# A dilated gated convolution: the last 16 channels summed by token, one of four products split further, and a new order of all steps

## The chip, the core and the metric

The kernel runs on one core of a Trainium2 chip. Its engines work side by side, each through its own queue in order: TensorE (PE in the profile, its weight loads PEld), VectorE (DVE), ScalarE (ACT), GpSimd (POOL), and SyncE (SP), which here only issues DMAs. They tell each other of finished work by semaphores. The metric is device time of one execution in microseconds; lower is better.

## The reference

```python
B, T, D, K = 2, 16000, 144, 15
dil, pad = 2, (K - 1) * 2
xp = jnp.pad(x, ((0, 0), (pad, 0), (0, 0)))
h = sum over i of einsum('btc,cd->btd', xp[:, pad - 2*i : pad - 2*i + T], w[i])   # w[i]: 144 x 288
z = jnp.tanh(h[..., :D]) * sigmoid(h[..., D:])
return z @ w_o                                                                    # w_o: 144 x 144
```

A causal convolution with 15 taps, each 2 tokens apart, from 144 to 288 channels; a gate; a projection. Everything is bf16, sums are held in f32.

## The kernel before, in words

Even and odd tokens never meet in the convolution, so each parity is a plane of its own with taps 1 apart. Per plane there are 8000 positions per batch, cut into groups of 24 positions. A block is 128 groups of one plane; there are 10 such blocks, and a last block of 32 groups of both planes. `load_x` brings the first 128 channels of a block to SBUF with a transposing DMA (channels on partitions); `gather` copies the last 16 channels to a DRAM tensor `xr`, and `load_r` reads that with overlapping rows, so that one transposing DMA puts 8 taps times 16 channels on 128 partitions (`rx`).

A unit is 12 of a group's 24 positions for all 128 groups, so there are 20 units (r is 0 or 1) and one for the last block. With 12 outputs and 15 taps a unit is computed as four smaller products, named S, D, F and G, from sums and differences of inputs 8 or 16 apart. F and G give outputs 8 to 11 and 0 to 3 together with U = (S + D)/2, and (S − D)/2 is outputs 4 to 7. The names S, D, E are also those of the sums on VectorE (`derive`, line 271), E serving F and G; a 2 or a 4 behind the name is a sum of neighbours 2 or 4 apart, an r is the same over `rx`.

Each product (`conv`) is again split, over taps 4 apart and then 2 apart, in these steps, which the plan knows by name:

- VV: 2 matmuls into one half of a PSUM pair X. cVV (line 507): ACT copies it negated into the other half.
- V2a, V2b: 2 matmuls on each half. cV (line 513): ACT copies both halves, negated, into another pair Y.
- A: for each of the four halves of X and Y, 4 matmuls (3 where a tap is missing) with the 128-channel sums, and 1 with the r sums.

Every matmul has 128 x 128 inputs as weights and 288 columns of w. There are four PSUM pairs in all, handed out in the order of the plan. For S and D the pairs are evicted by ACT into `m` (line 570), and VectorE makes y of outputs 4 to 7 and U from `m`; for F and G VectorE adds the pair to U (y) and so frees it. A gate is tanh, sigmoid and a product (z) over four outputs, three gates per unit. z is transposed by a DMA (`zT`, line 603), and the projection (OP0, OP1, line 343) is 24 matmuls with 144 columns, evicted by ACT into `os` (line 678) and stored.

All of this is written down as steps with a cost, the steps they depend on, and a `want`, a due time. `Plan.place` is a list scheduler: it goes through the engines with these costs and takes, among the steps that could start soonest, the one with the smallest `want`; so it sets the order on PE, ACT and DVE and who gets which PSUM pair. In the kernel before, `want` is worked out from a table of a unit's sequence (`SEQ`) and a unit length TU of 14.0. Transfers from SP are issued in an order that the scheduler of the framework may still move, except those held in program order.

For the last block ACT first spreads the inputs out (`spread_out`, line 328, 8 copies), so that groups of both planes stand side by side.

The prologue loads w, makes sums of taps (G1, Gm, H, HH: partly on VectorE, line 407, partly on TensorE by matmuls with the identity, `psum_sum`), and runs 48 matmuls on zeros. Unit 0 has an order of its own.

Of the kernel before, what the change touches and what calls it, by code (L numbers as in the profile page):

```python
# [11 lines left out]
ALU = mybir.AluOpType  # L12
# [14 lines left out]
def t_dve(n, psum=False):  # L27
    return 0.07 + n / (960 if psum else 1920)

# [32 lines left out]
class Plan:  # L62
# [4 lines left out]
    def __init__(self, n_slots):  # L67
        self.steps, self.n_slots = [], n_slots

    def add(self, eng, cost, fn, r=(), w=(), u=(), want=0.0, opens=None, pairs=(), name="", lat=None, behind=()):  # L70
# [3 lines left out]
        s.idx = len(self.steps)  # L74
# [15 lines left out]
        s.deps, s.behind = deps, set(behind) - deps  # L90
        for p in pairs:
            p.users.append(s)
        self.steps.append(s)
        return s

# [57 lines left out]
def kernel(  # L153
# [25 lines left out]
    TU = 14.0  # L179
# [36 lines left out]


    xn_b, rx_b = buf("xn", [P, XW], 2), buf("rx", [P, XW], 2)
    xr = dram.tile([2, NPOS, CR], BF16, name="xr")
    xr_g = {}  # L220
    blk = [dict() for _ in blocks]

    def plane(t_, bi, i):
        _, n, _, _ = geometry(bi)
        return t_[:, i * (HA + n):(i + 1) * (HA + n)]

    def load_x(bi, want, half=None, behind=()):

        p0, n, planes, _ = geometry(bi)
        if half != 1:  # L230
            blk[bi]["xn"] = xn_b.new(bi)
        g = blk[bi]["xn"]
        if half is not None:
            blk[bi]["xn", half] = Gen(g.before)
        gs = [g] if half is None else [g, blk[bi]["xn", half]]
        a, m = (0, HA + n) if half is None else ((0, HA + n // 2), (HA + n // 2, n // 2))[half]
        for i, e in enumerate(planes):
            v = plane(g.tile, bi, i)[:, a:a + m]
            loads, zeros = runs(p0 - HA + a, m)
            for c, m in zeros:  # L240
                add("POOL", 0.2, lambda v=v, c=c, m=m: nc.gpsimd.memset(v[:, c:c + m], 0.0), w=gs, want=want)
            for c, b, p, m in loads:
                src = bass.AP(x.tensor, x[b, 2 * p + e, 0].offset, [[2 * D, m], [1, P]])
                add("DMA", m * 0.0015, lambda v=v, c=c, m=m, src=src: nc.sync.dma_start_transpose(out=v[:, c:c + m], in_=src),
                    w=gs, want=want, name="xn", behind=behind)

    def gather(key, p0, n, planes, want, behind=()):
        g = xr_g[key] = Gen()
        loads, _ = runs(p0, n)
        for c, b, p, m in loads:  # L250
            e0, ne = planes[0], len(planes)
            src = bass.AP(x.tensor, x[b, 2 * p + e0, P].offset, [[2 * D, m], [D, ne], [1, CR]])
            dst = bass.AP(xr.tensor, xr[e0, FRONT + p0 + c, 0].offset, [[CR, m], [NPOS * CR, ne], [1, CR]])
            add("DMA", m * ne * 0.0013, lambda dst=dst, src=src: nc.sync.dma_start(out=dst, in_=src), w=[g], want=want, name="gather", behind=behind)

    def load_r(bi, want, keys):
        p0, n, planes, _ = geometry(bi)
        g = blk[bi]["rx"] = rx_b.new(bi)
        for i, e in enumerate(planes):
            v = plane(g.tile, bi, i)  # L260
            src = bass.AP(xr.tensor, xr[e, FRONT + p0 - HA - 7, 0].offset, [[CR, HA + n], [1, P]])
            add("DMA", (HA + n) * 0.0015, lambda v=v, src=src: nc.sync.dma_start_transpose(out=v, in_=src),
                r=[gz, *(xr_g[k] for k in keys)], w=[g], want=want, name="rx")
# [3 lines left out]
           "S2": (-4, 6), "D2": (-4, 6), "E2": (-12, 14), "Sr": (0, 8), "Dr": (0, 8), "Er": (-8, 16)}  # L267
    DER_B = {nm: buf(nm, [P, P * GEO[nm][1]], 2 if nm in ("E", "S4", "D4", "E4", "E2", "Er") else 1) for nm in GEO}

    def tt(out_, a, b, op):  # L270
        return K_(nc.vector.tensor_tensor(out=out_, in0=a, in1=b, op=op))  # L271

    def derive(bi, nm, want, half=None):
# [5 lines left out]
        k0, kn = (0, ns) if half is None else (half * (ns // 2), ns // 2)  # L279

        last = len(planes) == 2

        def cols(v, c, *dims):
            v = v[:]
            return bass.AP(v.tensor, v.offset + c, [list(v.ap[0]), *[list(d) for d in dims]])

        def go(g=g):
            if nm[-1] in "42":
                b0, bw = GEO[nm[0]]
                v, d = blk[bi][nm[0]].tile, int(nm[-1])  # L290
                a = [cols(v, (u0 - b0) * (ns if last else 1) + q, *([[1, wd * ns]] if last else [[bw, kn], [1, wd]])) for q in ((0, d * ns) if last else (k0 * bw, k0 * bw + d))]
                tt(cols(g.tile, 0, [1, wd * ns]) if last else cols(g.tile, k0 * wd, [wd, kn], [1, wd]), a[0], a[1], ALU.add)
                return
            t_ = blk[bi]["rx" if nm[-1] == "r" else "xn"].tile
            us = (u0, u0 + (16 if nm[0] == "E" else 8))
            if last:
                first = -8 if nm[-1] == "r" else -16
                lo, hi, o = *(cols(spread[nm[-1] == "r"], (u - first) * ns, [1, wd * ns]) for u in us), cols(g.tile, 0, [1, wd * ns])
            else:
                lo, hi = (cols(t_, HA + u + k0 * PU, [PU, kn], [1, wd]) for u in us)  # L300
                o = cols(g.tile, k0 * wd, [wd, kn], [1, wd])
# [5 lines left out]
        of = blk[bi][nm[0] if nm[-1] in "42" else "rx" if nm[-1] == "r" else "xn"]  # L307
        if last and nm[-1] not in "42":
            of = spread_g[nm[-1] == "r"]
        if half is not None and ("xn", half) in blk[bi]:  # L310
            of = blk[bi]["xn", half]
        add("DVE", t_dve(kn * wd), go, r=[of], w=[g], want=want, name=nm)

    spread = [const.tile([P, 40 * 64], BF16, name="xs"), const.tile([P, 32 * 64], BF16, name="rs")]
    spread_g = [Gen(), Gen()]

    def spread_out(bi, want):

        _, n, _, ns = geometry(bi)
        for i, (key, first, wd) in enumerate((("xn", -16, 40), ("rx", -8, 32))):  # L320
            for h in range(4):
                m = wd // 4

                def go(i=i, key=key, u=first + m * h, m=m, h=h):
                    a, b = blk[bi][key].tile[:], spread[i][:]
                    src = bass.AP(a.tensor, a.offset + HA + u, [list(a.ap[0]), [1, m], [HA + n, 2], [PU, ns // 2]])
                    dst = bass.AP(b.tensor, b.offset + h * m * ns, [list(b.ap[0]), [ns, m], [ns // 2, 2], [1, ns // 2]])
                    K_(nc.scalar.copy(out=dst, in_=src))  # L328

                add("ACT", t_act(m * ns), go, r=[blk[bi][key]], w=[spread_g[i]], want=want + 4 * i + h, name="spread")  # L330

    def stat(bi, r, nm, u):

        u0, wd = GEO[nm]
        v = blk[bi][nm].tile[:]
        ns = geometry(bi)[3]
        step, c = (1, (u - u0) * ns) if r is None else (wd, u - u0 + r)
        return bass.AP(v.tensor, v.offset + c, [list(v.ap[0]), [step, P]])
# [11 lines left out]
    HH = const.tile([P, 4, 2, D2], BF16)  # L350
    Wr = const.tile([P, 4, D2], BF16)
# [23 lines left out]
    zr = const.tile([64, 2, P], BF16)  # L375
    K_(nc.gpsimd.memset(zr[:], 0.0))
# [3 lines left out]


    gz = Gen()
    for q, (p0, m) in enumerate(((-FRONT, FRONT), (HP, GAP), (ENDP, NPOS - FRONT - ENDP))):
        dst = bass.AP(xr.tensor, xr[0, FRONT + p0, 0].offset, [[P, m * CR // P], [NPOS * CR, 2], [1, P]])
        add("ACT", 0.08, lambda dst=dst, m=m: nc.scalar.dma_start(out=dst, in_=zr[0:m * CR // P]), w=[gz], want=-30.5 if q == 0 else -25, lat=2.5)
# [50 lines left out]
    for i, k in enumerate("SD"):  # L436
# [4 lines left out]
        if k == "D":  # L441
# [4 lines left out]
            wsum(HH[:, i], H[:, i, 0:2], H[:, i, 2:4], ALU.subtract, [gH[k]], [gHH[k]], 0.9)  # L446
            continue
        psum_sum(HH[:, i], [plus(i, j) + minus(i, j + 4) + minus(i, j + 2) + plus(i, j + 6) for j in range(2)], wall, [gHH[k]], wt)
        psum_sum(H[:, i, 0:2], [plus(i, j) + minus(i, j + 4) for j in (0, 1)], wall, [gH[k]], wt + .2)
        psum_sum(H[:, i, 2:4], [plus(i, j) + minus(i, j + 4) for j in (2, 3)], wall, [gH[k]], wt + .1)  # L450
        psum_sum(g[:, 4:6], [plus(i, j) for j in (4, 5)], wall, [gG[k, 1]], wt + .3)
# [8 lines left out]


    y_b, m_b, U_b = buf("y", [P, NCL, D2], 2), buf("m", [P, 2, 4, D2], 2), buf("U", [P, 4, D2], 2)
    th_b, sg_b = buf("th", [P, 4, D], 3), buf("sg", [P, 4, D], 3)
# [3 lines left out]
    for z_ in z_b.tiles:  # L467
# [4 lines left out]
    SEQ = (("A0S", 1.22), ("V2D", .49), ("A1S", 1.22), ("VVF", .25), ("A0D", 1.22), ("V2F", .49), ("A1D", 1.22), ("VVG", .25),  # L472
           ("OP0", .75), ("A0F", 1.22), ("V2G", .49), ("A1F", 1.22), ("VVS'", .25), ("OP1", .75), ("A0G", 1.1), ("V2S'", .49),
           ("A1G", 1.22), ("VVD'", .25))
    SEQ0 = (("VVF", .25), ("VVG", .25), ("V2F", .49), ("A0F", 1.22), ("V2G", .49), ("A1F", 1.22), ("VVS", .25), ("A0G", 1.1),
            ("V2S", .49), ("A1G", 1.22), ("VVD", .25), ("A0S", 1.22), ("V2D", .49), ("A1S", 1.22), ("A0D", 1.22), ("VVS'", .25),
            ("A1D", 1.22), ("V2S'", .49), ("VVD'", .25), ("OP0", 0), ("OP1", 0))
# [9 lines left out]
    AT_ = {False: times(SEQ), True: times(SEQ0[:15] + (SEQ0[16],))}  # L487
# [320 lines left out]
```

## Time and profile before

| | us |
|---|---|
| median of 3 runs | 355.1 (354.83 to 355.15) |
| the profiled execution | 352.94 |
| its span, first to last instruction | 351.1 |
| PE, ACT, DVE busy in it | 324.0, 255.1, 243.5 |
| granted TensorE clock, mean | 0.988 |

A row of the timeline is start, length, engine, line, operation and out<-in with sizes; in brackets stands how long the engine was idle before it and what ended that. A row of a group ends in busy time, mean nanoseconds of one, idle time before them and its releasers. Matmuls overlap, so the length of one is longer than the step to the next; the step is what counts.

### The profile page before, as it was taken

Reading aid. Unit: us, or ns where it says so; the run is one execution under the profiler, and the core shown is the slowest. Engines: PE = TensorE matmul, PEld = TensorE weight load, DVE = VectorE, ACT = ScalarE, POOL = GpSimd, SP = SyncE. Lnnn points to the kernel's source line nnn. Section 1 sums busy time; section 2 is a strip of 40 time slices with the busy share of each in tenths; the row PEclk is TensorE's granted clock in tenths of the full one; section 3 lists DMA queues with packets and bytes.
Section 4 is the critical chain, followed back from the end, with each engine's and each line's share of the span. In section 5 each row is a group of like instructions: output and inputs, shape, how many; then the busy total and the mean of one; then the engine's idle time right before and its main releaser. Section 6 shows DMA issues by size and latency. Waiting matters only on the chain.

```text
span 351.1 us, 6812 instructions
## 1 busy us (share of the span) xinstructions
PE 324.0 (92%) x2754; PEld 302.7 (86%) x2754; DVE 243.5 (69%) x336; ACT 255.1 (73%) x448; POOL 21.8 (6%) x52
## 2 busy tenths in 40 slices
PE   8988596999999999999999999999988899999992
PEld 3678595899999899989989989998987889999881
DVE  3778966398697768939848794894877387385352
ACT  1256864686887687777677876767779997788883
POOL 8780000000000000000000000000000000000000
PEclk9999899999999999999999999999999999999996
DMA  9999999219349616426920833794090242202144
GB/s 192 225 82 62 117 212 192 52 40 193 54 169 191 109 21 141 93 54 246 191 54 1 149 86 85 204 200 54 1 140 0 54 202 54 54 1 54 29 131 157
DMA packets 140700, 38.17 MB, mean 109 GB/s; under 512 B 136995, under 2 KB 139347, under 8 KB 140670
## 3 DMA queue, kind: packets, MB, share of 16 engines
q1 hardware_dynamic: 136902, 35.94, 53.7%
q10 hardware_dynamic: 2744, 1.31, 1.4%
q0 software_dynamic: 1024, 0.51, 0.9%
q8 instruction: 21, 0.34, 0.4%
q14 instruction: 9, 0.07, 0.1%
HBM read 2.64 MB, written 10.25 MB: 37 GB/s over the span
## 4 chain that ended last, share of the span: by engine, by line
PE 48%; ACT 20%; DVE 17%; issue 7%; DMA 6%; ACTq 0%; DVEq 0%
PE acc L343 44%; DVE y L271 8%; DMA zT<-z 6%; DVE S L271 4%; PE acc L379 3%; ACT os L678 3%; ACT acc L513 3%; ACT th L550 3%; ACT sg L552 3%; ACT m L570 2%; DVE z L271 2%; ACT acc L507 2%; DVE U L271 1%; DVE Dr L271 1%; ACT xs L328 1%
## 5 line engine op out<-in xcount | busy, mean ns | idle before, releaser
L343 PEld LDWEIGHTS <-E 128*128 128x128 bf16 x882 | 111.6, 143 | 6.9 <-issue 4.1
L343 PE MATMUL acc<-w_all,E 128*128 128x288 bf16 x630 | 101.0, 286 | 0.7 <-ACT acc L513 0.5
L570 ACT ACTIVATE m<-acc 128x576 bf16<-128x576 f32 x84 | 53.9, 650 | 27.5 <-PE acc L343 26.9
L343 PEld LDWEIGHTS <-D 128*128 128x128 bf16 x462 | 58.6, 138 | 14.1 <-issue 12.9
L271 DVE TENSOR_TENSOR y<-U,acc 128x576 bf16<-128x576 bf16 x80 | 60.1, 751 | 12.1 <-PE acc L343 9.7
L550 ACT ACTIVATE th<-y 128x576 bf16<-128x576 bf16 (+1 forms) x64 | 43.3, 677 | 26.2 <-DVE y L271 25.3
L343 PEld LDWEIGHTS <-S 128*128 128x128 bf16 x462 | 57.4, 138 | 4.1 <-issue 3.5
L513 ACT ACTIVATE acc<-acc 128x576 f32<-128x576 f32 x84 | 54.0, 643 | 4.8 <-PE acc L343 4.3
L343 PE MATMUL acc<-Gm,D 128*128 128x288 bf16 x294 | 49.6, 289 | 8.3 <-ACT acc L513 7.2
L343 PE MATMUL acc<-G,S 128*128 128x288 bf16 x294 | 49.0, 286 | 2.2 <-ACT acc L513 2.0
L271 DVE TENSOR_TENSOR y<-m 128x1152 bf16<-128x1152 bf16 x21 | 15.9, 758 | 48.1 <-ACT m L570 48.1
L343 PE MATMUL acc<-Wr,Er 128*128 128x288 bf16 x168 | 47.4, 286 | 0.0
L552 ACT ACTIVATE sg<-y 128x576 bf16<-128x576 bf16 (+1 forms) x64 | 42.5, 666 | 0.0
L507 ACT ACTIVATE acc<-acc 128x288 f32<-128x288 f32 x84 | 33.9, 404 | 10.5 <-PE acc L343 10.3
L343 PE MATMUL acc<-wo_ab,zT 128*128 128x144 bf16 x480 | 35.8, 226 | 4.5 <-DMA zT<-z 4.5
L678 ACT CAST os<-acc 128x864 bf16<-128x864 f32 x40 | 34.3, 872 | 5.6 <-PE acc L343 5.3
L343 PEld LDWEIGHTS <-zT 128*128 128x128 bf16 x480 | 32.2, 98 | 6.5 <-DMA zT<-z 5.5
L271 DVE TENSOR_TENSOR z<-th,sg 128x576 bf16<-128x576 bf16 (+1 forms) x64 | 28.7, 448 | 8.2 <-ACT sg L552 7.9
L343 PE MATMUL acc<-H,E 128*128 128x288 bf16 x168 | 28.1, 288 | 1.5 <-ACT acc L507 1.5
L271 DVE TENSOR_TENSOR E<-E 128x1792 bf16<-128x1792 bf16 (+3 forms) x22 | 26.4, 1233 | 0.1
L343 PEld LDWEIGHTS <-Er 128*128 128x128 bf16 x168 | 23.9, 143 | 0.2
L343 PE MATMUL acc<-Wr,Sr 128*128 128x288 bf16 x84 | 24.0, 286 | 0.0
(73 smaller groups left out, 339.4 us busy)
## 6 DMA issues: line engine op xcount, KB each, us to landing
out_dram<-os SPq DMA_DIRECT2D x8, 864.0 KB
out_dram<-os SPq DMA_DIRECT2D x2, 519.8 KB
w_all<-in_w_dram ACTq DMA_DIRECT2D x3, 288.0 KB
out_dram<-os SPq DMA_DIRECT2D x2, 337.5 KB
xr<-in_x_dram SPq DMA_DIRECT2D x3, 192.0 KB
zT<-z SPq DMA_TRANSPOSE x20
xn<-in_x_dram SPq DMA_TRANSPOSE x15
Wr<-in_w_dram POOLq DMA_DIRECT2D x15, 9.0 KB, 4.4
```

The costliest lines, as they stand in the source:

```text
L271: return K_(nc.vector.tensor_tensor(out=out_, in0=a, in1=b, op=op))
L328: K_(nc.scalar.copy(out=dst, in_=src))
L343: K_(nc.tensor.matmul(bank, lhsT=l(), rhs=r, start=start and q == 0, stop=end and q == len(jobs) - 1, skip_group_check=True))
L379: K_(nc.tensor.matmul(banks[i % 4][:, (i // 4) % 2, :], lhsT=wz[:, 0:P], rhs=wz[:], start=True, stop=True))
L507: add("ACT", t_act(D2), lambda: K_(nc.scalar.activation(out=banks[X.slot][:, 1, 0:D2], in_=banks[X.slot][:, 0, 0:D2], func=ACT.Copy, scale ...
L513: s = add("ACT", t_act(2 * D2), lambda: K_(nc.scalar.activation(out=banks[Y.slot][:, :, 0:D2], in_=banks[X.slot][:, :, 0:D2], func=ACT.Cop ...
L550: add("ACT", t_act(n * D), lambda: K_(nc.scalar.activation(out=th.tile[:, 0:n], in_=yv[:, :, 0:D], func=ACT.Tanh)), r=[*need, y], w=[th], ...
L552: add("ACT", t_act(n * D), lambda: K_(nc.scalar.activation(out=sg.tile[:, 0:n], in_=yv[:, :, D:D2], func=ACT.Sigmoid)), r=[*need, y], w=[s ...
L570: add("ACT", t_act(2 * D2), lambda pair=pair, i=i, b2=b2: K_(nc.scalar.activation(out=m.tile[:, i, 2 * b2:2 * b2 + 2, :], in_=banks[pair.s ...
L678: K_(nc.scalar.copy(out=dst, in_=banks[pr.slot][:, :, 0:3 * D].rearrange("p h (q d) -> p h q d", d=D)))
```

## The change

1. **The last 16 channels.** `gather`, `load_r`, `xr` and the sums Sr, Dr, Er go. `load_t` loads those channels by token: one group per partition, 39 positions of 16 channels (`xt`). Three VectorE operations per block (`sums_t`) make the sums S, D and E on it; a transposing DMA puts them on channels (T), a DMA writes them to DRAM (q), and one DMA per unit reads them back as the 128 x 128 weights that the r matmuls need (R, three buffers).
2. **S split once more.** The A steps of S use sums S42 (of S4, 2 apart), 2 matmuls per half in place of 4, and a step AV of 4 matmuls with differences of taps 2 apart (GD) into a third pair; ACT evicts that into `av` (eAV), and VectorE adds it to `m` for even and subtracts it for odd outputs (av0, av1). D, F and G stay.
3. **The last block** is held twice in the sums, once for r = 0 and once shifted by one position, made by VectorE straight from `xn`, in two halves; `spread_out` goes.
4. **Joint gates.** Outputs 0 to 3 and 8 to 11 share one tanh, one sigmoid and one product of 8 outputs; the last unit keeps them apart.
5. **Order.** Each step's `want` is replaced by a number from a table (`PLACES`), by kind of unit: 0, 1, 2, the even and odd ones between (m0, m1), 18, 19, 20, and the prologue (p). TU is 13.2.

```diff
+PLACES = """
+    0: V2bG#0 -132.95 VVD#0 -131.98 av1#0 -120.52 U#0 -113.85 cVG#0 -113.17 A11D#0 -110.62 zm0#0 -106.16 y0F#0 -105.59 A11Gr#0 -105.28 VVS#0 -103.60
...
+    def places(self, unit_us):
...
+        for s in self.steps:
+            u = s.unit
+            kind = "p" if u < 0 else str(u) if u < 3 or u >= 18 else f"m{u % 2}"
+            n = seen[u, s.name] = seen.get((u, s.name), -1) + 1
+            s.want = max(u, 0) * unit_us + at[kind, f"{s.name or s.eng}#{n}"]
...
-    TU = 14.0
+    TU = 13.2
+    SPLIT = "S"
...
+    R_b = buf("R", [P, 4, 4, P], 3)
...
+        for k, m, i0, i1, b, p in groups:
+            src = bass.AP(x.tensor, x[b, 0, 0].offset + (p + 2 * i0) * D + P, [[2 * PU * D, m], [2 * D, i1 - i0], [1, CR]])
...
+            add("DMA", 0.05 + m * (i1 - i0) * 0.0007, lambda dst=dst, src=src: nc.sync.dma_start(out=dst, in_=src), r=[gz], w=[g], want=want, name="xt", behind=behind)
+
+    def sums_t(bi, want):
...
+        for k, (a, b), op in (("S", (8, 16), ALU.add), ("D", (8, 16), ALU.subtract), ("E", (16, 0), ALU.subtract)):
+            o = {"S": 0, "D": P, "E": 2 * P}[k]
+            n = P if k != "E" else 2 * P
+            add("DVE", t_dve(2 * n), lambda o=o, n=n, a=a, b=b, op=op: tt(ap(st.tile, o, [512, 2], [1, n]),
+                *(ap(g.tile, i * CR, [P, 2], [1, n]) for i in (a, b)), op), r=[g], w=[st], want=want, name="st" + k)
+        add("DMA", 1.4, lambda: nc.sync.dma_start_transpose(out=T.tile[:], in_=st.tile[:].rearrange("p k n -> p (k n)")), r=[st], w=[T], want=want + .1, name="T")
...
+            add("DMA", 1.8, lambda R=R, src=src: nc.sync.dma_start(out=R.tile[:].rearrange("p s k n -> p s (k n)"), in_=src), r=[q], w=[R], want=want + .3 + r, name="R")
...
+        split = k in SPLIT
+        if split:
+            W = Pair()
...
+            def go_av():
+                for h in range(2):
+                    mms(banks[W.slot][:, 1 - h, 0:D2], [job(st + "4", v - i - 4 * h, GD[:, SPLIT.index(k), h, i, :]) for i in range(2)])
...
+                for i in range(2 if split else 4):
+                    if split:
+                        wt = tap(k, 4 * h + i + (0 if c else 2))
+                        u = v - 4 * h - i - (0 if c else 2)
...
-                rest = [job(st + "r", v + 2 * c + 4 * b2, Wr[:, i4, :])]
-                parts = [(jobs, [g[st + "4"], *tap_gens(k)], 0), (rest, [g[st + "r"], gWr[k]], 2.5)]
+                rest = [job(k + "r", 2 * c + 4 * b2, Wr[:, i4, :])]
+                parts = [(jobs, [g[st + ("42" if split else "4")], *tap_gens(k)], 0), (rest, [g["R", r or 0], gWr[k]], 2.5)]
...
-            if not first and not (last and k == "G"):
-                gate(4 * j, 4, done(k, 1) + 1.0)
+            if last and k == "F":
+                gate(8, 4, done(k, 1) + 1.0)
+        if not first and not last:
+            gate(0, 8, done("G", 1) + 1.0)
...
+    plan.places(TU)
     for s in plan.place():
         s.fn()
```

More of the change, by code (lines that the diff above doesn't have):

```diff
@@ L31 @@
+"""
 class Gen:
@@ L73, in add @@
         s.lat = SEM[eng] if lat is None else lat
-        s.idx = len(self.steps)
+        s.idx, s.unit = len(self.steps), self.unit
         deps = set()
@@ L237, in load_x @@
         for i, e in enumerate(planes):
-            v = plane(g.tile, bi, i)[:, a:a + m]
+            v = g.tile[:, i * (HA + n) + a:i * (HA + n) + a + m]
             loads, zeros = runs(p0 - HA + a, m)
[L240 to L244, printed above, removed]
-                    w=gs, want=want, name="xn", behind=behind)
@@ L247, in gather @@
[L247 to L263, printed above, removed]
+            for c, m_ in zeros:
+                add("POOL", 0.2, lambda v=v, c=c, m=m_: nc.gpsimd.memset(v[:, c:c + m], 0.0), w=gs, want=want)
@@ L266 @@
     GEO = {"S": (-8, 16), "D": (-8, 16), "E": (-16, 24), "S4": (-8, 12), "D4": (-8, 12), "E4": (-16, 20),
[L267 to L271, printed above, removed]
+           "S2": (-4, 6), "D2": (-4, 6), "E2": (-12, 14), "S42": (-8, 10), "D42": (-8, 10), "E42": (-16, 18)}
@@ L273, in derive @@
+    DER_B = {nm: buf(nm, [P, P * GEO[nm][1]], 2 if nm[0] == "E" or nm[1:] == "4" else 1) for nm in GEO if nm[-2:] != "42" or nm[0] in SPLIT}
+    PART = {"4": "", "2": "", "42": "4"}
     def derive(bi, nm, want, half=None):
@@ L305, in go @@
                 tt(o, *((hi, lo) if nm[0] == "E" else (lo, hi)), ALU.subtract)
-        of = blk[bi][nm[0] if nm[-1] in "42" else "rx" if nm[-1] == "r" else "xn"]
-        if last and nm[-1] not in "42":
-            of = spread_g[nm[-1] == "r"]
+        of = blk[bi][nm[0] + PART[nm[1:]]] if nm[1:] in PART else blk[bi]["xn"]
         if half is not None and ("xn", half) in blk[bi]:
             of = blk[bi]["xn", half]
+        if last and nm[1:] not in PART:
+            for q in range(2):
+                add("DVE", t_dve(kn * wd // 2), lambda q=q: go(q), r=[of], w=[g], want=want, name=nm)
+            return
         add("DVE", t_dve(kn * wd), go, r=[of], w=[g], want=want, name=nm)
[L314 to L330, printed above, removed]
     def stat(bi, r, nm, u):
+        if nm[-1] == "r":
+            return blk[bi]["R", r or 0].tile[:, u // 2, KINDS.index(nm[0]), :]
         u0, wd = GEO[nm]
[L335 to L338, printed above, removed]
+        return ap(blk[bi][nm].tile, u - u0 + (r or 0), [wd, P])
     def mms(bank, jobs, start=True, end=True):
@@ L542, in gate @@
         def gate(c0, n, t0):
-            th, sg = th_b.new(gate.n), sg_b.new(gate.n)
-            gate.n += 1
-            need = [yg[c] for c in range(c0, c0 + n, 2)]
-            zs = [Gen(z.before) for _ in range(0, n, 2)]
-            zg.update(zip(range(c0, c0 + n, 2), zs))
-            yv = y.tile[:, c0:c0 + n, :]
-            add("ACT", t_act(n * D), lambda: K_(nc.scalar.activation(out=th.tile[:, 0:n], in_=yv[:, :, 0:D], func=ACT.Tanh)),
+            th, sg = (v[4 if n == 4 else 8].new(0) for v in (th_b, sg_b))
@@ L748 @@
     for ui, (bi, r) in enumerate(units):
+        plan.unit = ui
         base = ui * TU
```

305 lines of the change are left out of this document (224 added, 81 removed).

## The prediction

> **What bounds the kernel now.** I read the page's head and its chain first, then the busy times by stage, then single stretches of the timeline.
>
> ```profile
> span 351.1 us, 6812 instructions
> PE 324.0 (92%) x2754; PEld 302.7 (86%) x2754; DVE 243.5 (69%) x336; ACT 255.1 (73%) x448; POOL 21.8 (6%) x52
> PE 48%; ACT 20%; DVE 17%; issue 7%; DMA 6%; ACTq 0%; DVEq 0%
> ```
>
> TensorE is busy nearly always, yet holds only half of the chain; the other half is where it waits for a copy. How much it waits needs its pace:
>
> ```profile
> 195.45 0.53 PE L343 MATMUL acc<-Gm,D 128*128 128x288 bf16 x3
> 195.82 0.28 PE L343 MATMUL acc<-w_all,D 128*128 128x288 bf16 x1
> 57.32 1.67 PE L343 MATMUL acc<-wo_ab,zT 128*128 128x144 bf16 x24 [3.48 <-DMA zT<-z]
> 58.83 0.54 PE L343 MATMUL acc<-G,S 128*128 128x288 bf16 x3
> ```
>
> Three 288-column matmuls take 0.37 us, so 0.123 each; 24 of the projection take 1.51, so 0.063 each. A unit has 102 of the first and 24 of the second: 14.1 us, 0.1116 per matmul. Now the stages (prologue with units 0 and 1, regular units, one pair of them, the pair in which the last block is spread out, the end):
>
> ```profile
> 13.20:62.60 49.40, 39.20 (x307) 35.63 (x306) 37.82 (x46) 30.55 (x56) 9.77 (x18) 0.97 1.08 138
> 62.60:255.70 193.10, 187.43 (x1639) 182.32 (x1639) 144.04 (x195) 146.24 (x261) 0.42 (x3) 1.00 0.52 108
> 179.70:209.90 30.20, 29.07 (x254) 28.03 (x253) 22.35 (x30) 22.55 (x41) 0.00 (x0) 1.00 0.45 84
> 255.70:289.40 33.70, 29.86 (x252) 28.02 (x252) 22.87 (x31) 31.11 (x49) 0.00 (x0) 1.00 0.44 103
> 289.40:345.10 55.70, 55.14 (x508) 51.47 (x508) 32.65 (x57) 44.54 (x82) 0.00 (x0) 1.00 0.27 69
> ```
>
> First number is the length, the second PE busy with its matmuls, then PEld, DVE, ACT, POOL, granted clock. Length less matmuls times pace is lost time: 49.4 − 36.3 = 13.1 in the first stage (283 long, 24 short), 193.1 − 182.9 = 10.2 in the regular units (1.9 of it in the pair shown), 33.7 − 28.1 = 5.6 with the spread, where ACT is busy 31.1 of 33.7; at the end 0.6 by busy time. So about 30 us are waits, the rest is TensorE's own work.
>
> What a wait hangs on: each of the four products of a unit is a chain VV, negated copy (cVV), V2, negated copy (cV), A.
>
> ```profile
> 187.80 0.41 PE L343 MATMUL acc<-HH,S 128*128 128x288 bf16 x2
> 188.31 0.40 ACT L507 ACTIVATE acc<-acc 128x288 f32<-128x288 f32 x1 [0.20 <-PE acc L343]
> 19.45 0.46 ACT L507 ACTIVATE acc<-acc 128x288 f32<-128x288 f32 x1
> 19.96 0.65 PE L343 MATMUL acc<-H,E 128*128 128x288 bf16 x4 [1.00 <-ACT acc L507]
> 20.70 0.64 ACT L513 ACTIVATE acc<-acc 128x576 f32<-128x576 f32 x1 [0.80 <-PE acc L343]
> 21.39 1.14 PE L343 MATMUL acc<-w_all,E 128*128 128x288 bf16 x8 [0.54 <-ACT acc L513]
> ```
>
> From VV to its copy 0.51, the copy 0.40 and 0.05 to V2: 0.97 at least. From V2 to its copy 0.74, the copy with its handover 0.69: 1.43. PE needs other matmuls in between: six after VV's two, eight after V2's four. The cover fails when ACT's own order puts other work ahead of the copy:
>
> ```profile
> 193.06 0.65 PE L343 MATMUL acc<-H,D 128*128 128x288 bf16 x4
> 193.65 0.67 ACT L552 ACTIVATE sg<-y 128x576 bf16<-128x576 bf16 x1
> 194.23 0.63 ACT L570 ACTIVATE m<-acc 128x576 bf16<-128x576 f32 x1
> 194.76 0.64 ACT L513 ACTIVATE acc<-acc 128x576 f32<-128x576 f32 x1
> ```
>
> D's copy could start at 193.80 and starts at 194.76, behind a sigmoid and an eviction; A of D waits until 195.45. ACT steps are 0.53 to 0.58 here.
>
> **The change, term by term.**
>
> *TensorE's work.* S's A falls from 16 matmuls to 8 and gains 4 (AV): 4 fewer in each of 21 units, 84 × 0.123 = 10.3 us off the path, as PE is the bound in every stage but one. The prologue's GD adds 15 identity matmuls (59 for 44), 1.8 us on. Net −8.5.
>
> *ACT, DVE and the new order in regular units.*
>
> ```profile
> L550 ACT ACTIVATE th<-y 128x576 bf16<-128x576 bf16 x62 | 42.4, 685 | 26.2 <-DVE y L271 25.3
> L550 ACT ACTIVATE th<-y 128x288 bf16<-128x288 bf16 x2 | 0.9, 450 | 0.0
> L570 ACT ACTIVATE m<-acc 128x576 bf16<-128x576 f32 x84 | 53.9, 650 | 27.5 <-PE acc L343 26.9
> L271 DVE TENSOR_TENSOR Er<-rx 128x2048 bf16<-128x2048 bf16 x10 | 12.2, 1217 | 3.0 <-DMA rx<-xr 3.0
> L271 DVE TENSOR_TENSOR E<-E 128x1280 bf16<-128x1280 bf16 x1 | 0.8, 818 | 0.0
> ```
>
> A 1152-wide gate is 0.685 + 576 × 0.00082 = 1.16; in steps, two gates joined save about 0.1, and two pairs per unit 0.2. The new eviction of AV is 576 wide like m's, a step of 0.55. ACT gains 0.35 a unit on 11.3, against a unit of 14: covered. DVE loses Er, Sr, Dr (1.2 and about half that twice, 2.5 per block), gains S42 (0.82), three small sums (0.9) and two 576-wide adds per unit (0.45 each): about +0.5 per unit on 11.2, covered as long as U is out before the F products end. The adds stand between m and U, so 0.8 us later for every y; y frees the PSUM pairs for the next unit's VV.
>
> I walked the built order of one regular pair, matmul by matmul, with these durations and each engine's queue. Even unit: V2 of D is followed by VVF alone, two matmuls for eight, and VVF itself waits for S's eviction: 0.75 lost. A of F comes six matmuls after V2F: 0.3. Odd unit: VVD's copy is just covered by six; nothing else is missed, since the gates now stand behind the copies. 1.1 per pair, and 0.3 for gaps under 0.1 as before: 1.4 against 1.9, over 6.4 pairs 9.0 for 10.2, so −1.2. Bounds: all cover good, −10; each pair losing as now plus one more 0.8, +5.
>
> *The last block.*
>
> ```profile
> L328 ACT COPY xs<-xn 128x640 bf16<-128x640 bf16 x4 | 5.5, 1393 | 0.0
> L328 ACT COPY rs<-rx 128x512 bf16<-128x512 bf16 x4 | 4.6, 1145 | 0.0
> ```
>
> 10.1 us of ACT go, in the stage where ACT was full; in their place DVE makes its sums over copies held twice, and DVE has 10 us free there. What is left is a regular pair's loss: 5.6 to 2.0, −3.6 (bounds −5, 0).
>
> *The first stage.* This is where the change can hurt. SP's queue changes most: gathers and rx transposes go; xt loads, T, q and two R per block come, 121 instructions for 75.
>
> ```profile
> 2.84 9.42 SPq L244 DMA_TRANSPOSE xn<-in_x_dram  x2
> 12.39 4.10 SPq L262 DMA_TRANSPOSE rx<-xr  x1
> 11.93 0.96 DVE L271 TENSOR_TENSOR E<-xn 128x1536 bf16<-128x1536 bf16 x1 [0.91 <-DMA xn<-in_x_dram]
> 13.16 5.55 PE L343 MATMUL acc<-w_all,ident 128*128 128x288 bf16 x44
> 18.55 0.41 PE L343 MATMUL acc<-HH,E 128*128 128x288 bf16 x2
> 19.52 1.22 DVE L271 TENSOR_TENSOR Er<-rx 128x2048 bf16<-128x2048 bf16 x1 [2.97 <-DMA rx<-xr]
> 52.87 1.56 SPq L603 DMA_TRANSPOSE zT<-z  x1
> 0.00:30.00 30.00, 5.01 (x9) 1.41 (x2) 1.00 1.06 153
> ```
>
> (The last row is the weight sums alone.) In the built order xt0 is issued behind three xn transposes, so at about 11.5 (two of them are through at 12.26 here, with a gather ahead); a load under this traffic took from 4.4 (zT, 52.87 to 57.32) to 7.1 (rx, 12.39 to 19.5): xt0 lands near 16.5. On DVE the three sums on it stand ahead of Gm and of both halves of E. Behind them: 0.9, weight sums 3.8 (5.01 less H and HH, which come earlier), E 1.9: VVF can start at 23.1. PE is through 40 identity matmuls at 18.5: a wait of 4.6, none before. Bounds: xt0 landing by 11, 0; two hops late, 8.
>
> Then R: T after the sums at 17.5, 4.5 a hop, q 3.5, R behind the next block's xt: 29.5. PE reaches its first R product at about 29.7, so 0.5, at worst 8. Gaps of the chain in units 0 and 1 by the built order (V2F to A of F 1.1, unit 0's S and D 1.7, unit 1 2.0): 4.8. And the clock:
>
> ```profile
> 42.50 0.88 PE L343 MATMUL acc<-Gm,D 128*128 128x288 bf16 x3 [3.14 <-ACT acc L513]
> 42.50:45.60 3.10, 3.10 (x14) 2.24 (x14) 1.91 (x3) 1.32 (x3) 0.00 (x0) 0.53 1.05 179
> ```
>
> After an idle of 3.14 us the clock was at 0.53 for 14 matmuls, 1.4 us lost; after 3.48 idle at 57.32 the pace was full. I take the 1.4. [...] Sum of the stage: 4.6 + 0.5 + 4.8 + 1.4 = 11.3 for 13.1, −1.8: the 3.48 for zT goes, as unit 0's projection now stands two units later. Bounds −8, +10.
>
> *The end.* S gives less cover in the last three units, about 0.4 each: +1.2 (0 to +3). The gates of the last unit stay apart, so its tail stands.
>
> Sum: −8.5 − 1.2 − 3.6 − 1.8 + 1.2 = −13.9. The profiled execution took 352.94 (span 351.1 and 1.8 around it), 0.6% under the median of the runs, 355.1. 352.94 − 13.9 = 339.0; on the median **341.2**.
>
> **The rivals.**
>
> *Work only.* ACT's copies fall behind evictions in other places and the waits stay as long in sum: −8.5, **346.6**. For it: cover after S's copies shrinks from five-matmul groups to three. Against: ACT's largest block, the spread, is gone.
>
> *R late at the start.* xt of the next blocks stands ahead of q and R in SP's queue; if the R chain takes two hops more, 8 us, PE waits with all four PSUM pairs held: **349**. For it: four transfers in series where there were two. Against: PE itself is late through E.
>
> *Everything covered.* Regular pairs and the start lose half: **335**.
>
> *Slower: projections behind R in SP's queue.* The second R of a block waits until PE has finished the unit three before (three R buffers); a zT queued behind it starts late, and the projection stands in PE's line. A late zT costs what 57.32 shows, 3.48. By my walk zT lands some 3.5 us ahead of its use. It decides from about 5 us later: 1.5 lost in each of 9.5 pairs is 14; at 2 us in nine pairs, +18, **359**. Against: in the built order zT of an odd unit is issued ahead of that R.
>
> **How the numbers follow.** Forecast (336 to 345) 0.48; work only 0.20; R late 0.12; everything covered 0.09; slower 0.09; 0.02 for mixtures that end within 0.2% of 355.1, about what measurement can tell from no change. Faster 0.89, same 0.02, slower 0.09. The range 334 to 352 leaves out the slower case and the ends of the others.
>
> **What would show it.** In the changed profile: 2685 matmuls (2754 − 84 + 15); a pair of regular units 28.4 us long; VVF's first matmul at about 23 with DVE E ahead of it and xt behind that; slow clock just after; ACT below 27 of 34 us in the last block's pair; no wait of PE for zT over 0.5. Wrong if a regular pair lasts over 29.5, if PE waits for R beyond the start, or if zT's row shows PE waits in each pair.

## The result and the profile after

| | before | after |
|---|---|---|
| median, same chip | 354.97 (354.7 to 355.15) | 388.97 (388.36 to 389.85) |
| profiled execution, its span | 352.94, 351.1 | 388.94, 387.1 |
| mean granted clock | 0.988 | 0.917 |

The change made the kernel slower: ratio 1.096, 95% interval 1.0938 to 1.0983. The forecast was 341.2, faster.

The head of the changed kernel's page, some lines of its slices and of its chain (one slice is 9.7 us):

```profile
span 387.1 us, 6829 instructions
PE 315.0 (81%) x2685; PEld 289.1 (75%) x2685; DVE 253.8 (66%) x372; ACT 258.6 (67%) x423; POOL 24.8 (6%) x59
...
PE   8900053028899999999999999999999999999992
...
PEclk9965557558999999999999999999999999999998
DMA  9820140052667979889964996657985143541145
...
PE 55%; ACT 13%; DMA 12%; SPq 11%; DVE 4%; issue 4%; ACTq 0%; DVEq 0%
```

TensorE has its 2685 matmuls, as forecast, and from the tenth slice on it is at 8 or 9 tenths but for the last slice. The whole loss lies in the first 85 us: two holes in the PE row, in which the DMA row is almost empty too. The waits that belong to them (engine and line, what was waited for: us in total, times, longest):

```profile
DVE st L319 <- DMA xt<-in_x_dram: 33.8, 1, 33.8
...
PE acc L449 <- DVE E L319: 33.2, 1, 33.2
...
PE acc L449 <- DMA R<-q: 23.9, 1, 23.9
```

Each happens once. The chain through them (start, length, what):

```profile
13.37 32.09 DMA xt<-in_x_dram
...
45.54 0.83 DVE st L319 x3
...
46.39 3.27 DMA T<-st
...
49.68 1.49 SPq L389
...
51.62 29.71 SPq L376
...
81.43 3.46 DMA R<-q
...
84.93 5.69 PE acc L449 x23
```

The xt load of block 0, issued at 13.37, takes 32.09 us. VectorE's sums on it (`st`) stand in line ahead of Gm and E, so all of TensorE waits. Later an issue of line 376, the next xt instruction on SP's queue, is held for 29.71 us: a second load of the same form (block 1's) has just gone out in front of it, and the issues of both R stand behind. Stages of the changed kernel (length, then PE, PEld, DVE, ACT, POOL busy, granted clock, DMA share, GB/s); the first four are the two holes and what follows each, the fifth is one regular pair, the last the stretch from 100 to 380:

```profile
18.30:51.70 33.40, 0.25 (x3) 0.00 (x0) 5.99 (x12) 0.64 (x1) 7.83 (x16) 0.56 0.24 23
51.70:60.70 9.00, 8.38 (x49) 6.60 (x50) 8.86 (x11) 3.16 (x6) 0.00 (x0) 0.74 0.17 33
60.70:84.90 24.20, 0.31 (x3) 0.05 (x1) 3.99 (x3) 0.00 (x0) 0.00 (x0) 0.55 0.18 37
84.90:99.00 14.10, 12.42 (x75) 9.98 (x76) 1.50 (x3) 6.90 (x13) 0.00 (x0) 0.80 0.33 75
...
162.25:189.59 27.34, 27.23 (x246) 26.19 (x244) 23.71 (x37) 23.68 (x40) 0.00 (x0) 1.00 0.98 205
100.00:380.00 280.00, 275.69 (x2467) 263.01 (x2467) 230.26 (x339) 241.04 (x392) 2.40 (x7) 1.00 0.69 145
```

Behind the start the kernel came out better than forecast: a regular pair takes 27.34 us (30.20 before, 28.4 forecast). So the question is why a load of 155 KB takes 32 us.

### The profile page after: what moved, and what is told of

Its sections match the earlier page's. It is cut to its first block, busy times and chain, and to the rows that moved or that the text cites. A ratio compares the mean times of both kernels' runs of the same rounds, so it can differ in the third digit from the quotient of the medians.

```text
span 387.1 us, 6829 instructions
## 1 busy us (share of the span) xinstructions
PE 315.0 (81%) x2685; PEld 289.1 (75%) x2685; DVE 253.8 (66%) x372; ACT 258.6 (67%) x423; POOL 24.8 (6%) x59
## 4 chain that ended last, share of the span: by engine, by line
PE 55%; ACT 13%; DMA 12%; SPq 11%; DVE 4%; issue 4%; ACTq 0%; DVEq 0%
PE acc L449 55%; DMA xt<-in_x_dram 8%; SPq L376 8%; ACT acc L636 4%; SPq L342 3%; ACT m L714 3%; DMA zT<-z 2%; ACT os L831 2%; ACT th L697 1%; DVE y L319 1%; ACT sg L699 1%; DVE S L319 1%; ACT acc L630 1%; DMA R<-q 1%; DMA T<-st 1%
## 5 line engine op out<-in xcount | busy, mean ns | idle before, releaser
L449 PEld LDWEIGHTS <-E 128*128 128x128 bf16 x882 | 112.5, 145 | 41.4 <-DVE E L319 33.5
L449 PE MATMUL acc<-Wr,R 128*128 128x288 bf16 x336 | 95.9, 289 | 23.9 <-DMA R<-q 23.9
L449 PE MATMUL acc<-w_all,E 128*128 128x288 bf16 x630 | 102.9, 289 | 1.9 <-ACT acc L636 1.0
L319 DVE TENSOR_TENSOR y<-U,acc 128x576 bf16<-128x576 bf16 x80 | 60.0, 751 | 14.4 <-PE acc L449 13.2
L449 PEld LDWEIGHTS <-D 128*128 128x128 bf16 x462 | 58.6, 139 | 5.8 <-issue 3.6
L449 PEld LDWEIGHTS <-S 128*128 128x128 bf16 x378 | 48.1, 137 | 5.0 <-issue 2.4
L449 PEld LDWEIGHTS <-R 128*128 128x128 bf16 x336 | 33.2, 99 | 24.8 <-DMA R<-q 24.2
L449 PE MATMUL acc<-Gm,D 128*128 128x288 bf16 x294 | 48.9, 286 | 2.1 <-ACT acc L636 1.7
L449 PE MATMUL acc<-HH,E 128*128 128x288 bf16 x84 | 17.5, 291 | 33.2 <-DVE E L319 33.2
L697 ACT ACTIVATE th<-y 128x576 bf16<-128x576 bf16 (+2 forms) x44 | 38.9, 884 | 1.2 <-DVE y L319 0.9
L699 ACT ACTIVATE sg<-y 128x576 bf16<-128x576 bf16 (+2 forms) x44 | 38.8, 882 | 0.2 <-DVE y L319 0.2
L449 PE MATMUL acc<-wo_ab,zT 128*128 128x144 bf16 x480 | 36.6, 226 | 0.3 <-DMA zT<-z 0.3
L319 DVE TENSOR_TENSOR S<-xn 128x2048 bf16<-128x2048 bf16 (+1 forms) x12 | 13.6, 1137 | 33.2 <-PE acc L449 33.2
L449 PEld LDWEIGHTS <-zT 128*128 128x128 bf16 x480 | 32.7, 98 | 2.2 <-DMA zT<-z 0.6
L319 DVE TENSOR_TENSOR z<-th,sg 128x576 bf16<-128x576 bf16 (+2 forms) x44 | 25.7, 584 | 11.7 <-ACT sg L699 6.2
L319 DVE TENSOR_TENSOR st<-xt 128x256 bf16<-128x256 bf16 (+1 forms) x33 | 9.4, 332 | 33.8 <-DMA xt<-in_x_dram 33.8
L449 PE MATMUL acc<-G,S 128*128 128x288 bf16 x147 | 30.2, 286 | 1.4 <-ACT acc L636 1.1
L319 DVE TENSOR_TENSOR U<-m 128x1152 bf16<-128x1152 bf16 x21 | 15.9, 758 | 21.8 <-ACT m L714 21.5
## 6 DMA issues: line engine op xcount, KB each, us to landing
xt<-in_x_dram SPq DMA_DIRECT2D x6, 156.0 KB
```

The lines of the kernel that those rows point to most:

```text
L449: K_(nc.tensor.matmul(bank, lhsT=l(), rhs=r, start=start and q == 0, stop=end and q == len(jobs) - 1, skip_group_check=True))
L697: add("ACT", t_act(n * D), lambda: K_(nc.scalar.activation(out=a_, in_=y_[0], func=ACT.Tanh)), r=[*need, y], w=[th], want=t0, name=f"th{c0}")
L699: add("ACT", t_act(n * D), lambda: K_(nc.scalar.activation(out=b_, in_=y_[1], func=ACT.Sigmoid)), r=[*need, y], w=[sg], want=t0 + .1, name ...
```

## The experiments

Theory 1: block 0's and block 1's large xt loads cover 127 partitions, one of the 128 groups being cut at the batch's start and loaded by itself; the author's supposition is that the number of partitions decides how many of the 16 DMA engines share a load, and that 127, which has no divisor up to 16 but 1, leaves it to one. The prediction did not weigh it. Theory 2: the load is late because it stands behind three transposes in SP's queue. Theory 3: pieces of 32 bytes are that slow, whatever the rows. Theory 4: the searched order starves the start.

### The load by itself

> This kernel leaves out the whole computation: it copies x to the output and, before that, makes eleven loads one after the other on SP's queue, each started only when the one before has landed, into tiles of their own. Nine have the form of xt (rows of 32 bytes; 128, 127, 126, 112, 77, 49, 27 and 15 partitions of 39 pieces, and one of 1 x 24), two the form of 4 pieces of 288 bytes on 127 and on 128 partitions. Theory 1 (the number of partitions decides how many DMA engines share a load, and 127 has no divisor but 1): 127x39x16 takes about 32 us as the xt load of the changed kernel did (13.37, 32.09 long), 128x39x16 and 112x39x16 about 4 (2 us of fixed time and a sixteenth of 30), 126 (14 engines) about 4, 77 (11) and 49 (7) 4 to 5, 27 (9) and 15 (15) 2.5 to 3; 127x4x144 about 5, and longer than 128x4x144. [...] Theory 2 (the load stood behind the three transposes in SP's queue): alone, all of them take 2 to 5 us, 127 rows no longer than 128. Theory 3 (32-byte pieces are slow, whatever the rows): 128x39x16 takes 30 like 127x39x16, and the others in proportion to their rows (77: 18, 49: 12).

```diff
+    for n, (m, ni, c) in enumerate(((128, 39, 16), (127, 39, 16), (126, 39, 16), (112, 39, 16), (77, 39, 16), (49, 39, 16), (27, 39, 16), (15, 39, 16), (1, 24, 16), (127, 4, 144), (128, 4, 144))):
+        t = const.tile([P, ni * c], BF16, name=f"p{m}x{ni}x{c}")
...
+        if n:
+            K_(nc.vector.tensor_copy(out=t[0:1, 0:1], in_=seen[0:1, n - 1:n]))
+        K_(nc.sync.dma_start(out=dst, in_=src))
+        K_(nc.vector.tensor_copy(out=seen[0:m, n:n + 1], in_=t[0:m, 0:1]))
```

The groups of its page: one copy on VectorE per load, and behind the bar its own time, then how long VectorE waited for that load. A name is p, partitions, x, pieces.

```profile
L43 DVE COPY seen<-p127x39x 127x1 bf16<-127x1 bf16 x1 | 0.2, 156 | 30.6 <-DMA p127x39x<-in_x_dram 30.6
L43 DVE COPY seen<-p127x4x 127x1 bf16<-127x1 bf16 x1 | 0.2, 156 | 9.4 <-DMA p127x4x<-in_x_dram 9.4
L43 DVE COPY seen<-p126x39x 126x1 bf16<-126x1 bf16 x1 | 0.2, 156 | 4.6 <-DMA p126x39x<-in_x_dram 4.6
L43 DVE COPY seen<-p128x39x 128x1 bf16<-128x1 bf16 x1 | 0.2, 156 | 4.5 <-DMA p128x39x<-in_x_dram 4.5
L43 DVE COPY seen<-p112x39x 112x1 bf16<-112x1 bf16 x1 | 0.2, 157 | 4.2 <-DMA p112x39x<-in_x_dram 4.2
L43 DVE COPY seen<-p77x39x 77x1 bf16<-77x1 bf16 x1 | 0.2, 153 | 3.4 <-DMA p77x39x<-in_x_dram 3.4
L43 DVE COPY seen<-p49x39x 49x1 bf16<-49x1 bf16 x1 | 0.1, 148 | 3.2 <-DMA p49x39x<-in_x_dram 3.2
L43 DVE COPY seen<-p128x4x 128x1 bf16<-128x1 bf16 x1 | 0.2, 156 | 2.5 <-DMA p128x4x<-in_x_dram 2.5
...
L43 DVE COPY seen<-p1x24x 1x1 bf16<-1x1 bf16 x1 | 0.1, 144 | 2.3 <-DMA p1x24x<-in_x_dram 2.3
```

127 partitions take 30.6 us with nothing else in flight; 128 take 4.5 and 126 take 4.6. One partition more is a factor of 6.8, one fewer of 6.7. With pieces of 288 bytes the same holds (9.4 against 2.5). That is theory 1's pattern; theories 2 and 3 fall as explanations of the 32 us: nothing stood ahead, and the pieces of 128 and 127 rows are equal.

The trace also records every packet that the DMA engines moved. Behind the pieces of each load stand some packets of 4 bytes: 16, 1, 14, 16, 11, 7, 9 and 15 of them for 128, 127, 126, 112, 77, 49, 27 and 15 partitions. These are the numbers that theory 1 gives for the engines, each time; a packet's record has its queue but not its engine, so that one engine carries the slow load is the author's inference. The 4953 pieces of the slow load start one after another, 5.9 ns apart, over 29.2 us; the 4992 pieces of 128 partitions are through in 3.0 us. The 508 pieces of 288 bytes on 127 partitions start 15.9 ns apart, so a larger piece took longer, and the forecast of 5 us for them was too low. The smaller loads were somewhat quicker than forecast (3.4 and 3.2 for 77 and 49 partitions, 4 to 5 expected).

### The same kernel with 112 and 15 rows

> The changed kernel with one thing else: each xt load over 127 partitions is issued as two, over 112 and over 15 partitions (blocks 0 and 1); same bytes, same place in SP's queue, same order of everything else. Theory 1 (127 rows go over one DMA engine): the load that took 32.1 us takes about 5, the wait of 33.4 us before the first HH,E goes to 0 to 5 and the 24.1 us wait for R with it, since R's chain starts 28 us earlier and has nothing slow ahead of it; 335 to 340 us against 355. Theory 2 (the place behind the transposes in SP's queue) and theory 4 (the searched order starves the start): 385 to 390, both waits as before. Theory 3 (small pieces): 385 to 390.

```diff
-            src = bass.AP(x.tensor, x[b, 0, 0].offset + (p + 2 * i0) * D + P, [[2 * PU * D, m], [2 * D, i1 - i0], [1, CR]])
...
+            cuts = [(0, 112), (112, 15)] if m == 127 else [(0, m)]
+            def go_xt(k=k, i0=i0, i1=i1, b=b, p=p, cuts=cuts):
+                for o, n in cuts:
+                    src = bass.AP(x.tensor, x[b, 0, 0].offset + (p + 2 * i0 + o * 2 * PU) * D + P, [[2 * PU * D, n], [2 * D, i1 - i0], [1, CR]])
+                    dst = g.tile[k + o:k + o + n, i0 * CR:i1 * CR].rearrange("p (i c) -> p i c", c=CR)
+                    nc.sync.dma_start(out=dst, in_=src)
```

Median 337.95 us (335.91 to 340.65), against 354.99 for the kernel before on the same chip: ratio 0.9554, interval 0.9484 to 0.9623. One line of a DMA's shape is worth 51 us, and the change without it is faster than the kernel before. The order of the steps is the same in both runs, so theory 4 does not explain the loss either. The head, a piece of the chain and the waits of TensorE (lines lie 6 further down in this kernel and those below: L455 is the L449 above, L642 cV):

```profile
span 334.1 us, 6833 instructions
```

```profile
12.65 5.93 DMA xt<-in_x_dram
```

```profile
PE acc L455 <- DVE E L319: 6.2, 1, 6.2
PE acc L455 <- ACT acc L642: 3.8, 9, 0.8
```

The load takes 5.93 instead of 32.09, the first wait 6.2 (at most 5 was expected) instead of 33.2, and no wait for R is left. Of the 53.0 us between the spans (387.1 to 334.1) 27.0 + 23.9 are these two waits; the other 2.1 are of the size of what the slow clock cost behind them (0.74 and 0.80 in the two stages shown).

### One load at a time

> As the run with 112 and 15 rows, but for block 0 alone; block 1's xt load stays on 127 partitions. Theory 1: the wait before the first HH,E goes (33.4 to at most 5); the slow load of block 1 is still issued between block 0's sums and R, holds q's and R's issues back as before, and PE waits for R 24 us or more (up to 30, since it gets there earlier): 355 to 365 us. Theories 2, 3 and 4: no change, 389.

> As the run with 112 and 15 rows, but for block 1 alone; block 0's xt load stays on 127 partitions. Theory 1: the wait of 33.4 us before the first HH,E stays, the 24.1 us wait for R falls below 5: 362 to 370 us. If 24 us of R's wait were owed to the late start of R's chain itself (T, q and R each a hop after the late xt of block 0), it stays at 15 or more: 380 or more. Theories 2, 3 and 4: no change, 389.

```diff
-            cuts = [(0, 112), (112, 15)] if m == 127 else [(0, m)]
+            cuts = [(0, 112), (112, 15)] if m == 127 and bi == 0 else [(0, m)]
```

(and bi == 1; one execution each.) With only block 0's load cut: 364.8 us; the waits and the chain of it:

```profile
PE acc L455 <- DMA R<-q: 25.1, 1, 25.1
```

```profile
25.60 31.36 DMA q<-T
56.98 3.78 DMA R<-q
```

With only block 1's load cut: 362.6 us, and TensorE does not wait for R. So R's wait was not owed to the late start of its own chain.

```profile
PE acc L455 <- DVE E L319: 33.1, 1, 33.1
```

Each wait belongs to one load, and they add: 389.0 − 364.8 = 24.2 and 389.0 − 362.6 = 26.4 make 50.6, with both cut it was 51.0 (so close by luck: the four executions with both cut lie 4.7 us apart). The second load hurts though nobody needs its data yet: q, issued behind it at 25.60 and 3 to 5 us long in runs without the slow load, lands 31.36 us later, and for 29.61 of these SP is still at q's issue.

### The slow load on another queue

> As the run where only block 0's xt load is cut (364.8, TensorE waits 25.3 us for R behind block 1's load over 127 rows), but that one load is issued from ScalarE's queue instead of SP's. If the slow load holds only what stands behind it on its own queue: the wait for R at about 35 us falls below 3. If it holds the DMA engine that every other transfer needs a sixteenth of: the wait stays above 20 and the time at 360 to 366. In the first case block 1's xt still takes 31 us from its issue at about 30, so its sums, R and the S products of unit 2 come about 15 us late: 345 to 355 in all.

```diff
-                    nc.sync.dma_start(out=dst, in_=src)
+                    (nc.scalar if n == 127 else nc.sync).dma_start(out=dst, in_=src)
```

349.8 us. Waits of TensorE, then the chain:

```profile
PE acc L455 <- DVE S L319: 7.9, 1, 7.9
...
PE acc L455 <- DMA R<-q: 2.1, 1, 2.1
```

```profile
18.55 42.04 DMA xt<-in_x_dram
```

R's wait falls from 25.1 to 2.1, so in these runs the slow load held what stood behind it on its own queue (q, 31.36 us), and hardly another queue's transfers. It lasts 42.04 us now, and block 1's sums come late for it (7.9).

### The place in SP's queue

> The run with 112 and 15 rows, where block 0's xt loads stand on SP's queue ahead of the transpose of block 1 (third in the queue) instead of behind it, with their memset earlier on POOL; T, q and both R then stand ahead of block 1's xt as well. Order of TensorE, VectorE and ScalarE as before. If the rest of the wait at the start (6.4 us before the first HH,E, VectorE idle 8.1 us for xt) is the place behind that transpose, whose issue takes 6.2 us, xt lands near 11 instead of 18.6 and the wait falls below 1 us: 331 to 333 beside 338. If VectorE's chain of sums is late anyhow (weights, xn), the wait falls to 4 and the time to 336. If the transposes that follow are held up in turn (block 1's E late): no gain, 338 or more.

```diff
+    order = plan.place()
+    xns = [s for s in order if s.name == "xn"][:3]
+    xts = [s for s in order if s.name == "xt" and s in blk0_xt.writers]
+    first = [d for s in xts for d in s.deps if d.eng == "POOL"][:1] + xns[:2] + xts + xns[2:]
+    for s in first + [s for s in order if s not in first]:
+        s.fn()
```

(block 0's xt and block 1's transpose are also held in program order on SP.) 331.51 us (329.95 to 331.62), ratio to the kernel before 0.9366, interval 0.933 to 0.9402: the fastest version here. A row of VectorE's timeline and one of TensorE's waits:

```profile
15.04 0.83 DVE L319 TENSOR_TENSOR st<-xt 128x256 bf16<-128x256 bf16 x3 [4.06 <-DMA xt<-in_x_dram]
```

```profile
PE acc L455 <- DVE E L319: 2.5, 1, 2.5
```

xt lands near 15, not at 11 as expected, and the wait goes from 6.2 to 2.5; the span falls by 4.5 (334.1 to 329.6), the median by 6.4. In the five runs with the table of places where block 0's cut load keeps its old place the wait lies between 6.2 and 9.2, so the profiled execution with 112 and 15 rows is the best of these. The place behind the transpose, theory 2, is real, at about a tenth of the loss; this run also moves a memset and puts T, q and both R ahead of block 1's xt, and these were not taken apart.

### Other odd rows

> The run with 112 and 15 rows, with the xt loads of the later blocks cut as well, wherever the number of rows is odd: 77 into 64 and 13, 49 into 48 and 1, 27 into 16 and 11. Only SP's queue gets more instructions. [...] If a load on 7 or 11 engines delayed q, R or zT behind it in the regular units, some of the short waits for zT go: 334 to 336. If the added issues on SP cost: 340 or more.

```diff
-            cuts = [(0, 112), (112, 15)] if m == 127 else [(0, m)]
+            cuts = {127: [(0, 112), (112, 15)], 77: [(0, 64), (64, 13)], 49: [(0, 48), (48, 1)], 27: [(0, 16), (16, 11)]}.get(m, [(0, m)])
```

336.9 us, inside the range of the run with 112 and 15 rows alone. Loads on 77, 49 and 27 rows cost 3.4 us or less by themselves and their data is wanted a block later. So this run does not tell how much faster such loads become by themselves.

### The split of S, the order and the gates

> The run with 112 and 15 rows, with one more thing undone: S's private products are whole again in every unit (16 matmuls instead of 8 and 4; no eviction of AV, no two adds, no S42; the 15 identity matmuls for GD stay). The placed order is given the same places. If TensorE's own work is the bound, 84 matmuls of 0.123 us come back: 10.3, so 348 us beside 338 for the run it is built on. If the split costs cover (what VVF and VVD wait for, the adds ahead of U), part of it is given back: 342 to 346. If the split was worth nothing because ACT or DVE bound the units: 336 to 340.

> The run with 112 and 15 rows, without the table of searched places: the planner orders the same steps by its own due times, as it did in the kernel before. If the searched order is what brought the regular units from 1.6 us lost per pair to 0.3, about 1.3 x 10 pairs come back and with the start some 5: 345 to 357. If the joint gates and the last block's copies alone did it: 336 to 342. Theory 4 (the searched order starves the start) asked for less than the run it is built on: below 334.

> 112 and 15 rows, S's products whole, and no table of places: beside the run without places (390.5, S split) it shows what the split is worth in the planner's own order. If TensorE's work decides: 84 matmuls of 0.123 more, 400 us. If the split costs cover there (the run without places loses 1.7 us in each pair between GD,S and Gm,D, waiting for an eviction): those 10 x 1.7 go and the work comes back, 380 to 386. If it costs more than it saves in every unit (pairs of PSUM banks held by AV as well): 360 to 378, close to the kernel before.

> 112 and 15 rows, no table of places, S split, and the two gates of a unit that the change joined are apart again (576 wide each). If the joint gate's long steps (1.16 us instead of two of 0.69 at their own times) hold evictions back in the planner's order, this is faster than the 390.5 of the run it is built on: 375 to 386. If joining only saves ACT its fixed time (0.2 us a unit, off the path): 389 to 392. If it saves on the path: 394 or more.

```diff
-        split = k in SPLIT
+        split = False
...
-            sp = [k for k in SPLIT if k in "SD"]
+            sp = []
...
-    plan.places(TU)
```

(The first two edits make S whole, the third takes the table away; the fourth run puts two gates of four outputs in the place of the joint one.) Times in us, all with 112 and 15 rows. The two in the column of the table are medians of four executions, with ratios 0.9554 and 1.0339 (1.0311 to 1.0366) to the kernel before; the others are one execution each:

| | table of places | planner's own due times |
|---|---|---|
| S split | 337.95 | 390.5 |
| S whole | 365.4 | 364.3 |
| S split, gates apart | not tried | 396.4 |

TensorE's wait for cV (L642) in the run without table and S split; in the one without table and S whole; in the one with table and S whole:

```profile
PE acc L455 <- ACT acc L642: 36.7, 44, 1.6
```

```profile
PE acc L455 <- ACT acc L642: 6.0, 11, 0.7
```

```profile
PE acc L455 <- ACT acc L642: 10.8, 20, 0.8
```

With the planner's own due times the split makes the kernel 26 us slower, although TensorE has 84 matmuls fewer; with the table it makes it 27 us faster. TensorE waits 36.7 us for cV in 44 places without the table, 3.8 us in 9 with it. With the table S whole was expected to cost 10.3 us at most and cost 27; without the table the case that the split costs more than it saves (360 to 378 expected) came. Taking the table away was expected to give 357 at most and gave 390.5. By the profiles, the wait for E apart, TensorE waits 18.6 us with the table and S whole against 6.7 with the split; with the 10.3 of the matmuls that is most of the 27. Without the table one place shows how the split loses: from 200.92 ScalarE does a joint tanh, a joint sigmoid and an eviction, then the copy cV at 203.70, and TensorE waits 1.61 us for it. The right-hand column cannot be compared with the left without care: the table was made for the split, so 365.4 is a bad order for S whole and not the best there is (the kernel before, with an order for S whole and gates apart, took 355). With the gates apart the planner's own order took 6 us longer, where 0.2 per unit off the path was forecast. With one execution each on two chips, and 4.7 us between the executions of one run above, that gain is not shown; with the table it stays open.

## Why the prediction was wrong, point by point

**The step that failed** is the landing of xt0 in the first stage: "a load under this traffic took from 4.4 (zT, 52.87 to 57.32) to 7.1 (rx, 12.39 to 19.5): xt0 lands near 16.5", with bounds for the wait from 0 to 8. Both rows are transposes, of another form, and their durations were carried over to a load whose shape, 127 partitions of 39 pieces, stood in the code. It took 32.09, and the wait was 33.2 for a forecast of 4.6. The bound "two hops late" multiplied the same wrong price. The probe shows what the number of partitions did: 30.6 us on 127, 4.5 on 128 and 4.6 on 126.

**R**: "29.5 ... so 0.5, at worst 8" was 23.9. The prediction had seen that R stands behind the next block's xt, and its rival "R late at the start" named this place; the price, 8, came from the same hop. What it had wrong is how long a load ahead can hold the queue: block 1's held SP for 29.71 us, though nobody waited for its data. The two waits are 28.6 and 23.4 over their terms, 52.0 together, of which the rest of the kernel gave some 4 back.

**First stage without these loads**: forecast a wait for E of 4.6 and VVF at 23; with 112 and 15 rows xt0 lands at 18.6 for 16.5, the wait is 6.2 and E is done at 25.5. R's wait, forecast 0.5, does not appear. The mechanism (xt behind three transposes, VectorE's line behind xt) was right, as moving it shows. The slow clock afterwards came, and cost more than the 1.4 taken: 0.74 over 9.0 us, some 2.3, behind 33 us of idling, and 0.70 over 8.5 us, some 2.5, behind the wait of 6.2.

**Regular pairs**: forecast 28.4, measured 27.34; 244 matmuls (98 of 0.123 and 24 of 0.063 per unit) are 27.1, so 0.2 is lost, not 1.4. The walk had V2 of D followed "by VVF alone, two matmuls for eight". The timeline after:

```profile
169.87 0.65 PE L449 MATMUL acc<-H,D 128*128 128x288 bf16 x4
170.35 0.91 PE L449 MATMUL acc<-wo_ab,zT 128*128 128x144 bf16 x12
171.10 0.41 PE L449 MATMUL acc<-HH,E 128*128 128x288 bf16 x2
171.37 0.66 PE L449 MATMUL acc<-Gm,D 128*128 128x288 bf16 x4
```

Half a projection, 12 matmuls, stands between, and A of D starts on time; the walk overlooked it.

**Last block and end**: the stretch from 62.6 to 345.1 before lost 10.2 + 5.6 + 0.6 = 16.4 by the prediction's count, and the forecast for it was 9.0 + 2.0 + 1.8 = 12.8. That count puts the end in by busy time and the rest by pace. By 0.123 for a long and 0.063 for a short matmul, the 282.5 us before hold 1904 and 494 and lost 17.2; the 280 us shown after hold 1950 and 517 and lost 7.6. So the gain was some 6 us larger than forecast, mostly in the pairs; the two stretches do not hold quite the same steps, so this is an estimate. The two units in which the last block was spread out ended 510 matmuls before the end; with 12 fewer behind them, they are this stage of the run with 112 and 15 rows:

```profile
245.60:272.90 27.30, 27.19 (x246) 26.14 (x245) 22.24 (x30) 23.64 (x40) 0.00 (x0) 1.00 0.32 81
```

It is as long as a regular pair. ACT is busy 23.64 of 27.30 us in it (31.11 of 33.70 before): below the 27 named, and TensorE is covered.

**TensorE's work**: 2685 matmuls, as counted. But "84 × 0.123 = 10.3 us off the path" treated the split and the order as terms that add. They don't: without the order the split loses 26 us. What the rival "work only" feared (copies falling behind evictions in other places) is seen in that case, at a far larger price than the rival gave it.

**The rivals**: no wait for zT came in the pairs, so the forecast's slower case did not happen; the kernel was slower by a wait whose place the rival "R late" had and whose size no rival held. Without the two slow loads the forecast would have stood: 337.95 against 341.2, inside its range, with the start some 3 us worse and the rest some 6 us better than forecast. So the nearness is in part two errors that cancel.

## What to carry to other kernels

Read the shape of every new DMA, not only its bytes and its place in the queue: 154.8 KB on 127 partitions took 30.6 us alone, 156.0 KB on 128 took 4.5. Where a load has such a count of partitions, try it alone and in parts (112 + 15 for 127 cost one more issue per load and gave 51 us). A slow transfer can cost what stands behind it on its queue, even where its own data is not needed yet: block 1's load held SP for 29.71 us, and TensorE waited 23.9 for R. A saving of work on the bounding engine that shortens its cover is no term of its own: cost it together with the order that it runs in.

## What the runs showed of the hardware

- 127 partitions of 39 pieces of 32 bytes: 30.6 us alone; 128 partitions: 4.5; 126: 4.6; 112: 4.2. With pieces of 288 bytes, 4 per partition: 9.4 on 127, 2.5 on 128.
- By the packets of that run, the loads on 128, 127, 126, 112, 77, 49, 27 and 15 partitions end in 16, 1, 14, 16, 11, 7, 9 and 15 packets of 4 bytes, the numbers that theory 1 gives for the engines. On 127 partitions the pieces of 32 bytes start 5.9 ns apart, those of 288 bytes 15.9 ns.
- With a load of this kind ahead, q on SP's queue landed 31.36 us after its issue had begun; with the load on ScalarE's queue TensorE waited only 2.1 us for R, and the load took 42.04 itself.
